# A delta-rule attention with a gated feed-forward: first feed-forward tiles in plain fp32, weights unpacked with byte copies, 32-blocks solved whole

## The chip, the cores and the metric

The kernel runs on one core of a Trainium2 chip. PE is TensorE, DVE is VectorE, ACT is ScalarE, POOL is GpSimd and SP is the engine that issues most transfers. The metric is the device time of one execution, in microseconds. The time before is the median of three runs; one more execution was profiled, and its page, trace and rows by line are what the text quotes. The prediction's sum is made against the profiled execution.

## The reference

The kernel computes two things in a row. The first is a delta-rule recurrence for 4 x 8 heads of 768 steps and width 48. The second is a feed-forward layer over the 3072 resulting tokens (width 384), with a hidden width of 2048.

```python
k_n = k / (np.linalg.norm(k, axis=-1, keepdims=True) + 1e-06)
for t in range(S):
    y[:, :, t] = np.einsum('bhd,bhde->bhe', q[:, :, t], state)
    v_old = np.einsum('bhde,bhd->bhe', state, kt)
    state = state + bt[:, :, :, None] * np.einsum('bhd,bhe->bhde', kt, vt - v_old)
# x: y laid out as (tokens, 384)
h = x @ w_in                                   # 384 -> 2048
g = where(h >= 1, h, where(h <= -1, 0.0, (h + 1) ** 2 / 4))
out = g @ w_out                                # 2048 -> 384
```

The two weight matrices arrive in 64-bit floating point; q, k, v and beta are 32-bit.

## The kernel before, in words

The sequence is cut into twelve chunks of 64 steps; two chunks form a group, so there are six groups G = 0 to 5. Within a chunk the recurrence becomes a triangular system. `gram_k` and `gram_q` form products of keys with keys and of keys with queries. `lanes` transposes the diagonal 32-blocks so that each of the 128 partitions holds one block, computes the norms and scales. A solve then inverts the blocks on DVE, one column after another, and an `unlanes` routine transposes them back. In groups 0 and 1 (`G < WHOLE`) the solve works on two 16-blocks at once (`solve`, 15 steps), and `merge16_a` and `merge16_b` join them on PE; from group 2 on `solve_whole` (30 steps) inverts 32-blocks. `merge32_a` and `merge32_b` join 32-blocks to 64. The chain over chunks is `chain_r` (read the state), `chain_u` (solve for the updates), `chain_y` (outputs, which become the x of the feed-forward layer) and `chain_d` (update the state).

The feed-forward layer is worked off in items `(G, f, bs)`: f is one of sixteen tiles of 128 hidden units, bs says which of the group's two chunks the item covers (256 columns each). An item is an up-projection (`up`, PE, result h), a gate (ACT and DVE, result s), a split of s into a rounded high half and a low half (`rest`, results ghi and glo), and a down-projection (`down`, PE, result o, two items later). Weights and activations are held as a high and a low half in the type fp32r, and each product is three passes (`PASSES`: high x high, high x low, low x high). Group 0 begins with six items on the first chunk alone (`LEAD`), goes on with ten on both, and ends with six on the second chunk.

The 64-bit weights are turned into fp32 on the chip by `weight(f)`, per tile and half: ACT scales the upper words (L149), POOL multiplies by zero what is left of them in place (L150), DVE shifts and joins words (L152, L154), ACT rounds to the high half (L158), DVE subtracts to get the low half (L160). Ten tiles are loaded at the start (`HOLD`), six later.

The order of the work is written out by hand. The opening, before the first item, is a list of `stage(...)` calls with weight steps filled in (`run(wu, n)`); while DVE solves, PE runs `KEEP` dummy matmuls (L518, plain fp32, 512 columns). From the first item on, `plan(G)` puts each piece of the next group's recurrence at a place counted in items from the group's start: `at(pe, G, t, ...)` for products on PE, `at(fill, G, t, ...)` for steps of the generators and loads. All engines work off their instructions in the order in which they are issued. x reaches its place partly by transfers from a staging tile (`stg`, six per chunk), issued by SP, for chunk 0 half of them by ACT.

The gate before, in the loop over items (relu is ACT; max is DVE):

```python
relu(s[:, c], h[:, c], half, -0.5)
relu(s[:, c], s[:, c], one, -1.0)
nc.scalar.activation(out=s[:, c], in_=s[:, c], func=AF.Square)
nc.vector.tensor_tensor(out=s[:, c], in0=h[:, c], in1=s[:, c], op=ALU.max)
```

Of the kernel before, what the change touches and what calls it, by code (L numbers as in the profile page):

```python
# [22 lines left out]
KEEP = 18  # L23
PASSES = ((0, 0), (0, 1), (1, 0))
WHOLE = 2
HOLD = 10
LEAD = 6
LAG = 2


@with_exitstack
def delta_rule_moe(ctx: ExitStack, tc: tile.TileContext, kqa, kqb, kv, beta, w, out):
# [88 lines left out]
    weight_loads(2, HOLD)  # L121
# [20 lines left out]

    def weight(f):

        x = X4[:, f % 4]
        st = RAW.pop(f)
        sti, xi = st.bitcast(I32), x.bitcast(I32)
        h, l = (sti[:, :, k::2] for k in (1, 0))
        nc.scalar.mul(out=x, in_=st[:, :, 1::2], mul=2.0 ** -112)  # L149
        nc.gpsimd.tensor_scalar(out=st[:, :, 1::2], in0=st[:, :, 1::2], scalar1=0.0, scalar2=None, op0=ALU.mult)  # L150
# [3 lines left out]
        nc.vector.scalar_tensor_tensor(out=xi, in0=xi, scalar=3, in1=l, op0=ALU.logical_shift_left, op1=ALU.bitwise_or)  # L154
# [3 lines left out]
        nc.scalar.copy(out=hi, in_=x)  # L158
        yield
        nc.vector.tensor_tensor(out=lo, in0=x, in1=hi, op=ALU.subtract)  # L160
        yield


# [70 lines left out]
    ZT = XT[:, :, :, 0:32]  # L234

    def lanes(G):

        A = S["A"] = sb.tile([P, 32, 32], F32, name="A", bufs=1)
        if G < WHOLE:
            X = S["X"] = sb.tile([P, 2, 16, 16], F32, name="X", bufs=1)  # L240
            Xf = X.rearrange("l s c t -> l (s c t)")
# [22 lines left out]
        if G >= WHOLE:  # L264
            nc.vector.scalar_tensor_tensor(out=A, in0=A, scalar=-1.0, in1=gm[:, :, None].broadcast_to([P, 32, 32]), op0=ALU.mult, op1=ALU.mult)  # L265
            nc.gpsimd.affine_select(out=A, in_=A, pattern=[[-1, 32], [1, 32]], base=0, channel_multiplier=0,  # L266
                                    compare_op=ALU.is_gt, fill=0.0)
            nc.gpsimd.memset(A.rearrange("l c t -> l (c t)")[:, 0:1024:33], 1.0)
            return
        A16 = S["A16"] = sb.tile([P, 2, 16, 16], F32, name="A16", bufs=1)  # L270
        for s in range(2):
            b = slice(16 * s, 16 * s + 16)
            nc.vector.tensor_tensor(out=A16[:, s], in0=A[:, b, b], in1=gm[:, b, None].broadcast_to([P, 16, 16]), op=ALU.mult)
        X32 = S["X32"] = sb.tile([P, 32, 32], F32, name="A", bufs=1)
        nc.gpsimd.memset(X32, 0.0)
        yield

    def solve():

        X, A16 = S["X"], S["A16"]  # L280
        for j in range(15):
# [2 lines left out]
            nc.vector.tensor_tensor(out=pr, in0=X[:, :, 0:n, j:j + 1].broadcast_to([P, 2, n, m]),  # L284
                                    in1=A16[:, :, j:j + 1, j + 1:16].broadcast_to([P, 2, n, m]), op=ALU.mult)
            nc.vector.tensor_tensor(out=X[:, :, 0:n, j + 1:16], in0=X[:, :, 0:n, j + 1:16], in1=pr, op=ALU.subtract)
# [493 lines left out]
```

## Time and profile before

| what | value |
|---|---|
| median of 3 runs | 640.39 us (640.23 to 642.42) |
| profiled execution | 640.92 us |
| its span | 639.2 us |
| mean granted PE clock | 0.946 |
| PE, DVE, ACT, POOL busy | 582.3, 451.9, 387.6, 101.6 us |
| first up-projection of group 0, 1, 2 | at 73.15, 213.81, 299.83 us |
| first up-projection of group 5 | at 566.50 us |

The span is what the trace covers, from the first instruction to the last; the execution's time is 1.7 us longer. In a view of stretches, each row gives the stretch's length and then each engine's busy time with the number of instructions, the granted clock of PE as a share of full speed, the DMA engines' share and GB/s. In a view of groups by line, a row gives the busy time in all and the mean of one in nanoseconds, then the engine's idle time just before such instructions and what ended it. In a timeline, a row gives the start and the length; a bracket gives the idle time before it and what ended that. Each plain fp32 matmul shows as two records.

### The profile page before, as it was taken

The page shows a single profiled execution, that of the slowest core. Times are in us where ns is not written, and L with a number is a line of the kernel's source. Part 1 is how long each engine was busy: PE and PEld are TensorE (multiplying, and loading weights), DVE is VectorE, ACT ScalarE, POOL GpSimd, SP SyncE. Part 2 cuts the span into 40 slices and gives each one's busy share as a digit, 9 for nine tenths or more (in the row PEclk, how much of TensorE's full clock was granted, in tenths as well). Part 3 has the DMA queues.
Part 4 walks back from the last instruction along what each step waited for, and adds up shares of the span by engine and source line. Part 5 has one row for each costly group of instructions (what it writes and reads, how often), then busy time and mean ns, then how long its engine had stood idle before and what let it go on. Part 6 is the DMA issues. An engine that isn't in the chain of part 4 may idle for free.

```text
span 639.2 us, 21003 instructions
## 1 busy us (share of the span) xinstructions
PE 582.3 (91%) x9158; PEld 499.8 (78%) x9158; DVE 451.9 (71%) x921; ACT 387.6 (61%) x696; POOL 101.6 (16%) x119
## 2 busy tenths in 40 slices
PE   9944588897988999999999999999999999999996
PEld 7443477676877787888987888978888878899995
DVE  6999479795486598785897866997948973533332
ACT  4145567753664766656766657656667577566663
POOL 3458525300000400001200004000012000000000
PEclk9955689697999999999999999999999999999998
DMA  7914353000014210015210043200052000010002
GB/s 241 417 48 151 120 184 110 1 26 3 4 28 125 84 50 28 2 40 168 73 31 4 2 121 90 74 27 4 24 147 79 11 3 2 19 45 14 1 2 49
DMA packets 21100, 42.35 MB, mean 66 GB/s; under 512 B 4624, under 2 KB 10128, under 8 KB 21008
## 3 DMA queue, kind: packets, MB, share of 16 engines
q1 hardware_dynamic: 20144, 40.14, 20.4%
q8 instruction: 72, 1.18, 0.8%
q10 hardware_dynamic: 608, 0.79, 0.4%
q0 software_dynamic: 256, 0.08, 0.1%
q14 instruction: 20, 0.16, 0.1%
HBM read 33.91 MB, written 4.72 MB: 60 GB/s over the span
## 4 chain that ended last, share of the span: by engine, by line
PE 53%; DVE 32%; ACT 6%; issue 5%; DMA 1%; ACTq 0%; POOL 0%; SPq 0%; DVEq 0%
PE o L583 20%; PE h L568 18%; PE ch L175 8%; DVE glo L693 4%; DVE pr L295 3%; DVE A L297 3%; DVE s L723 3%; PE ch L420 3%; PE ch L358 2%; ACT ghi L692 2%; DVE wt L152 2%; ACT WQ L200 2%; DVE xb L154 2%; DVE pr L284 1%; DVE XT L305 1%
## 5 line engine op out<-in xcount | busy, mean ns | idle before, releaser
L568 PE MATMUL h<-xb,wt 128*128 128x512 f32 (+1 forms) x918 | 227.0, 392 | 9.3 <-DVE s L723 4.8
L583 PE MATMUL o<-wt,ghi 128*128 128x384 f32 x768 | 202.8, 346 | 0.8 <-ACT ghi L692 0.8
L568 PEld LDWEIGHTS h<-xb,wt 128*128 128x128 f32 x918 | 165.6, 192 | 42.4 <-DVE s L723 6.4
L583 PEld LDWEIGHTS o<-wt,ghi 128*128 128x128 f32 x768 | 138.1, 190 | 8.3 <-ACT ghi L692 1.5
L583 PE MATMUL o<-wt,glo 128*128 128x384 f32 x384 | 130.8, 341 | 0.0
L723 DVE TENSOR_TENSOR s<-h,s 128x512 f32<-128x512 f32 (+1 forms) x102 | 66.8, 655 | 89.6 <-ACT s L715 89.1
L692 ACT CAST ghi<-s 128x512 fp32r<-128x512 f32 (+1 forms) x102 | 60.8, 596 | 87.1 <-DVE s L723 77.6
L693 DVE TENSOR_TENSOR glo<-s,ghi 128x512 fp32r<-128x512 f32 (+1 forms) x102 | 68.7, 673 | 47.4 <-ACT ghi L692 46.0
L697 ACT ACTIVATE s<-h,half 128x512 f32<-128x512 f32 (+1 forms) x102 | 67.4, 661 | 50.7 <-PE h L568 50.0
L583 PEld LDWEIGHTS o<-wt,glo 128*128 128x128 f32 x384 | 73.0, 190 | 0.9 <-DVE glo L693 0.9
L697 ACT ACTIVATE s<-s,one 128x512 f32<-128x512 f32 (+1 forms) x102 | 71.4, 700 | 2.4
L715 ACT ACTIVATE s<-s 128x512 f32<-128x512 f32 (+1 forms) x102 | 61.9, 607 | 3.2
L208 POOL TENSOR_SCALAR_AFFINE_SELECT WQ<-WQ 64x512 f32<-64x512 f32 x48 | 34.2, 712 | 95.8 <-ACT WQ L200 93.3
L150 POOL TENSOR_SCALAR wt<-wt 128x768 f32<-128x768 f32 x16 | 39.2, 2454 | 41.6 <-ACT xb L149 41.2
L297 DVE TENSOR_TENSOR A<-A,pr 128x30 f32<-128x30 f32 (+14 forms) x120 | 40.9, 341 | 4.4
L295 DVE TENSOR_TENSOR pr<-A 128x30 f32<-128x30 f32 (+14 forms) x120 | 40.1, 334 | 1.4
L266 POOL TENSOR_SCALAR_AFFINE_SELECT A<-A 128x1024 f32<-128x1024 f32 x4 | 5.1, 1268 | 200.4 <-DVE A L265 200.4
L404 ACT COPY SU<-ch 64x384 f32<-64x384 f32 x46 | 21.8, 473 | 14.8 <-PE ch L175 14.1
L200 ACT COPY WQ<-ch 64x512 f32<-64x512 f32 x40 | 23.2, 580 | 7.4 <-PE ch L175 6.6
L420 PEld LDWEIGHTS ch<-WQ,SU 112*64 112x64 f32 x704 | 21.6, 138 | 4.6 <-ACT SU L404 3.4
L456 DVE TENSOR_TENSOR SU<-ch,SU 48x384 f32<-48x384 f32 x40 | 22.2, 555 | 3.4 <-PE ch L175 2.7
L420 PE MATMUL ch<-WQ,SU 112*64 112x64 f32 x704 | 23.1, 224 | 1.1 <-ACT SU L404 1.1
(130 smaller groups left out, 617.1 us busy)
## 6 DMA issues: line engine op xcount, KB each, us to landing
wt<-in_w_dram SPq DMA_DIRECT2D x16, 768.0 KB, 7.9
KV<-in_kv_dram SPq DMA_DIRECT2D x24, 384.0 KB, 4.5
out_dram<-wx SPq DMA_DIRECT2D x47, 96.0 KB, 2.2
WQ<-in_kqb_dram SPq DMA_DIRECT2D x24, 128.0 KB, 3.2
WK<-in_kqb_dram SPq DMA_DIRECT2D x24, 96.0 KB, 3.5
WQ<-in_kqa_dram SPq DMA_DIRECT2D x22, 96.0 KB, 2.8
xb<-X SPq DMA_DIRECT2D x63, 32.0 KB, 2.0
WK<-in_kqa_dram SPq DMA_DIRECT2D x20, 96.0 KB, 3.4
```

The lines of the kernel that those rows point to most:

```text
L150: nc.gpsimd.tensor_scalar(out=st[:, :, 1::2], in0=st[:, :, 1::2], scalar1=0.0, scalar2=None, op0=ALU.mult)
L175: nc.tensor.matmul(tiles[i][dst:dst + l.shape[-1], v], l, r, start=True, stop=True)
L295: nc.vector.tensor_tensor(out=pr, in0=A[:, 0:n, j:j + 1].broadcast_to([P, n, m]), in1=A[:, j:j + 1, j + 1:32].broadcast_to([P, n, m]), op= ...
L297: nc.vector.tensor_tensor(out=A[:, 0:n, j + 1:32], in0=A[:, 0:n, j + 1:32], in1=pr, op=ALU.add)
L420: nc.tensor.matmul(yy[tk:tk + C, v // NP, v % NP], SF[rows, u:u + C], w_[rows, h, v, :], start=True, stop=True)
L568: nc.tensor.matmul(h[:, cols(bs)], WT[f][:, 0, x, k * P:(k + 1) * P], XB[G][:, y, k, cols(bs)], start=(n == 0), stop=(n == 8))
L583: nc.tensor.matmul(oacc[G, k], (ghi, glo)[x][:, k * P:(k + 1) * P], WT[f][:, 1, y, :], start=(new and n == 0), stop=(left[G, b] == 0 and n ...
L692: nc.scalar.copy(out=ghi[:, c], in_=s[:, c])
L693: nc.vector.tensor_tensor(out=glo[:, c], in0=s[:, c], in1=ghi[:, c], op=ALU.subtract)
L697: nc.scalar.activation(out=out, in_=in_, func=AF.Relu, bias=bias, scale=scale)
L715: nc.scalar.activation(out=s[:, c], in_=s[:, c], func=AF.Square)
L723: nc.vector.tensor_tensor(out=s[:, c], in0=h[:, c], in1=s[:, c], op=ALU.max)
```

## The change

- **Plain fp32.** The first eight tiles (`PLAIN = 8`), for the items of group 0 that cover the first chunk or both, multiply fp32 weights `W32` with fp32 x (`X32`) in one plain product instead of three passes; their s goes to the down-projection as it is. `split_x` later makes the high and low halves of group 0's x, and `rework` those of the eight tiles (a copy, a rounding, a subtraction each), from the tenth item on.
- **Unpacking.** `parts(f)` is three ACT operations: the top three bits of the lower word by way of its highest byte, a byte copy of sign and exponent, and the scaling of the upper word. `words(f)` is two DVE operations. POOL's pass is gone. All sixteen tiles are loaded at the start; `parts` of twelve of them (`HOLD = 12`) are issued in one row before the first solve.
- **Solve.** Every group uses the 32-block solve; the 16-block routines are gone. Before it stand a scaling of the whole tile on DVE and two POOL operations.
- **Gate.** One relu, the square, and one DVE operation of two steps (min with 1, max with h).
- **Pieces.** `chain_d(0)`, `chain_r(1)` and loads of group 2 move from the first items into the opening. The places of all pieces are new lists (`FIRST`, `OPEN`, `SECOND`, `STEADY`), the solve of a group is spread over its own stretch (`spread`), and `PRE` and `PACE` say how many weight steps run where. `KEEP` grows from 18 to 26.
- **Smaller things.** `merge32_b` gives its first two evictions to ACT and its last two to DVE instead of taking turns; the zeroing of XT is done once, by POOL; `copy` with `ONE` (all zeros) leaves the copies on DVE.

The diff, cut to its core:

```diff
-KEEP = 18
+KEEP = 26
-WHOLE = 2
-HOLD = 10
+HOLD = 12
+PLAIN = 8
...
-    weight_loads(2, HOLD)
+    weight_loads(2, FT)
...
+    def parts(f):
+        st = RAW[f]
+        by, wd = st.bitcast(U8), st.bitcast(I32)
+        nc.scalar.activation(out=wd[:, :, 0::2], in_=by[:, :, 3::8], func=AF.Identity, bias=floor, scale=2.0 ** -5)
+        nc.scalar.copy(out=by[:, :, 3::8], in_=by[:, :, 7::8])
+        nc.scalar.mul(out=st[:, :, 1::2], in_=st[:, :, 1::2], mul=2.0 ** -112)
+    def words(f):
+        wd = RAW[f].bitcast(I32)
+        rest_, top = wd[:, :, 0::2], wd[:, :, 1::2]
+        nc.vector.tensor_scalar(out=rest_, in0=rest_, scalar1=7 - 2 ** 31, scalar2=None, op0=ALU.bitwise_and)
+        yield
+        y = RAW[f][:, :, 0:DM] if f < PLAIN else X2[:, f % 2]
+        nc.vector.scalar_tensor_tensor(out=y.bitcast(I32), in0=top, scalar=3, in1=rest_, op0=ALU.logical_shift_left, op1=ALU.bitwise_or)
+        W32[f] = y
+        yield
+    def halves(f, x):
+        both_ = const.tile([P, 2, 2, DM], F32R, name=f"wt{f}")
+        hi, lo = (both_[:, :, i, :] for i in range(2))
+        nc.scalar.copy(out=hi, in_=x)
+        yield
+        nc.vector.tensor_tensor(out=lo, in0=x, in1=hi, op=ALU.subtract)
...
+    def rework():            # per tile f < PLAIN: copy to x = X2[:, f % 2], then halves(f, x)
+                nc.vector.tensor_copy(out=x, in_=W32[f])
...
+    def split_x():           # per k: high half on ACT, low half on DVE
...
+    PRE = [0, 0, 2, 0, 0, 1, 4, 2, 2]
...
+    for f in range(HOLD):
+        parts(f)
     run(solve())
     run(unlanes())
-    stage(one_(merge16_a, 0), (wu, 3))
...
+    run(wu, next(W))
+    stage(one_(merge32_a, 0), (sv[0], 2), (wu, next(W)))
+    stage(one_(merge32_a, 1), (wu, next(W)))
     late_q()
+    stage(one_(merge32_b, 0), (wu, next(W)))
+    stage(one_(merge32_b, 1), (sv[1], 2), (wu, next(W)))
+    stage(one_(chain_u, 0), (wu, next(W)))
+    stage(both(chain_y, 0), (wu, next(W)))
     load_k(2)
     load_q(2)
+    stage(one_(chain_d, 0), (wu, next(W)))
+    load_kv(2)
+    stage(one_(chain_r, 1), (wu, next(W)))
+    load_k(3)
...
+    def plain(G, f, bs):
+        return G == 0 and f < PLAIN and bs != (1,)
...
+            if plain(G, f, bs):
+                nc.tensor.matmul(h[:, cols(bs)], W32[f][:, 0, k * P:(k + 1) * P], X32[:, k, cols(bs)], start=(k == 0), stop=(k == 2))
+                continue
...
+    FIRST = dict(ln=[3.5, 3.5, 4.0, 4.0, 4.5, 5.0, 5], so=[6.0, 10], un=[10.5, 11.0, 11.5, 12.0], va=[7.5, 7.5], vb=[12.0, 13.5], r=[7.5], m=[12, 12, 13, 13], kt=[7.5], K=[14, 15.0], T=[17.0, 18, 18.5, 19, 19.5, 20, 20.5], Q=[21.5, 23.5])
+    OPEN = dict(I=[0, 0.5, 1, 1.5, 2, 6.5, 6.0], L=[2.5, 2.5], X=[2.0, 2.5, 3.5, 4.5, 4.5, 5.0], W=[10.0, 0.5])
+    SECOND = dict(ln=[-7.5, -6.5, -6.0, -4.5, -3.5, -3.5, -3.0], so=[-2.5, 5.0])
+    STEADY = dict(ln=[-5.5, -5, -5, -4.0, -4.0, -2.5, -2.5], so=[-0.5, 5.0], un=[5.5, 6.0, 6.0, 6.5], va=[2.0, 5.0], vb=[9.0, 10.0], r=[9.0], m=[8, 8.5, 8.5, 9.5], kt=[7.5], K=[10, 10.5], T=[11.0, 11.5, 12.0, 12.5, 13.0, 13.5, 15.5], Q=[17.0, 18.0])
...
-        relu(s[:, c], h[:, c], half, -0.5)
+        relu(s[:, c], h[:, c], half, 0.5)
...
-        relu(s[:, c], s[:, c], one, -1.0)
+        run(wu, pace(n, 0))
...
-        nc.vector.tensor_tensor(out=s[:, c], in0=h[:, c], in1=s[:, c], op=ALU.max)
+        nc.vector.scalar_tensor_tensor(out=s[:, c], in0=s[:, c], scalar=1.0, in1=h[:, c], op0=ALU.min, op1=ALU.max)
```

`PACE` gives the weight steps before and after each item's square: 5, 2 for the first item, mostly 2, 2 after it; by it all sixteen tiles are in words before the ninth item.

More of the change, by code (lines that the diff above doesn't have):

```diff
@@ L160, in weight, with unpack @@
         nc.vector.tensor_tensor(out=lo, in0=x, in1=hi, op=ALU.subtract)
+        WT[f] = both_
         yield
+    def unpack():
+        last = None
+        for f in range(FT):
+            if HOLD <= f + 1 < FT:
+                parts(f + 1)
+            yield from words(f)
+            if f >= PLAIN:
+                split = halves(f, W32.pop(f))
+                next(split)
+                if last:
+                    next(last)
+                yield
+                last = split
+        if last:
+            next(last)
+    def rework():
+        last = None
+        for f in range(PLAIN + 1):
+            if f < PLAIN:
+                x = X2[:, f % 2]
+                nc.vector.tensor_copy(out=x, in_=W32[f])
+                W32.pop(f)
+                split = halves(f, x)
+            if last:
+                next(last)
+                yield
+                next(last)
+            yield
+            last = split
+    def split_x():
+        XB[0] = sb.tile([P, 2, 3, 2 * NB], F32R, name="xb")
+        for k in range(3):
+            nc.scalar.copy(out=XB[0][:, 0, k], in_=X32[:, k])
+            yield
+            nc.vector.tensor_tensor(out=XB[0][:, 1, k], in0=X32[:, k], in1=XB[0][:, 0, k], op=ALU.subtract)
+            yield
     pairs = ((0, C, C, 0), (C, 0, 0, 1))
@@ L520, in delta_rule_moe @@
     run(ln)
+    for q, r in enumerate(QS):
+        for x in range(2):
+            nc.gpsimd.dma_start(out=beta_sb[r + 16 * x:r + 16 * x + 16, 1:NS, :], in_=beta[q:64:4, 2 + x:ntot:2, :])
+    for f in range(HOLD):
+        parts(f)
     run(solve())
@@ L573, in down @@
         ghi, glo = gs.pop((G, f, bs))
+        passes = [((ghi, glo)[x], WT[f][:, 1, y]) for x, y in PASSES] if glo else [(ghi, W32[f][:, 1])]
         for b in bs:
@@ L581, in down @@
                     new = False
-                for n, (x, y) in enumerate(PASSES):
-                    nc.tensor.matmul(oacc[G, k], (ghi, glo)[x][:, k * P:(k + 1) * P], WT[f][:, 1, y, :],
-                                     start=(new and n == 0), stop=(left[G, b] == 0 and n == 2))
+                for n, (x, y) in enumerate(passes):
+                    nc.tensor.matmul(oacc[G, k], x[:, k * P:(k + 1) * P], y, start=(new and n == 0),
+                                     stop=(left[G, b] == 0 and n == len(passes) - 1))
     def store(G, b):
@@ L655, in plan, with steps @@
-        if G < NS - 2:
-            at(fill, G, L, (load_kt, b + 2))
-            at(fill, G, R + 0.5, (load_k, a + 2))
-            at(pe, G, K[0], one(gram_k, a + 2))
-            at(pe, G, K[1], one(gram_k, b + 2, KT))
+        p, q = (STEADY if G else FIRST), (FIRST, SECOND, STEADY)[min(G, 2)]
+        def steps(gen, ts):
+            for t in ts:
+                at(fill, G, t, (gen, 1))
+        steps(lanes(G + 1), q["ln"])
+        spread(G, solve(), *q["so"])
+        steps(unlanes(), p["un"])
@@ new lines, in plan @@
+        steps(scale_v(a), p["va"])
+        steps(scale_v(b), p["vb"])
+        if G == 0:
+            I = OPEN["I"]
+            at(pe, G, I[0], one(chain_u, 1))
+            at(pe, G, I[1], *both(chain_y, 1))
+            at(pe, G, I[2], one(chain_d, 1))
+            for t, f, g in zip(I[3:], (gram_k, gram_k, gram_q, gram_q), (a, b, a, b)):
+                at(pe, G, t, one(f, g))
+            at(fill, G, OPEN["L"][0], (load_q, 3))
+            at(fill, G, OPEN["L"][1], (load_kv, 3))
+            steps(split_x(), OPEN["X"])
+            rw, (t, d) = rework(), OPEN["W"]
+            steps(rw, [t + int(j * d * 2) / 2 for j in range(2 * PLAIN + 1)])
```

255 lines of the change are left out of this document (70 added, 185 removed).

## The prediction

> **What bounds the kernel now.** I read the page's head first, then the busy times by stage, cut where the work changes hands.
>
> ```profile
> span 639.2 us, 21003 instructions
> ```
>
> ```profile
> 31.09:45.08 13.99, 6.81 (x512) 6.39 (x512) 13.75 (x16) 6.47 (x9) 7.77 (x3) 0.62 0.20 79
> 45.08:59.45 14.37, 5.95 (x258) 4.77 (x259) 13.99 (x19) 7.76 (x15) 11.30 (x11) 0.50 0.32 101
> 59.45:73.15 13.70, 6.54 (x126) 5.87 (x127) 10.64 (x18) 7.38 (x15) 9.84 (x8) 0.62 0.43 136
> ```
>
> ```profile
> 73.15:213.81 140.66, 119.84 (x2491) 102.51 (x2491) 98.42 (x203) 80.98 (x161) 28.23 (x32) 0.90 0.24 70
> ```
>
> ```profile
> 213.81:299.83 86.02, 84.48 (x1287) 73.16 (x1285) 67.84 (x148) 56.24 (x102) 7.47 (x13) 1.00 0.15 45
> 299.83:388.72 88.89, 87.69 (x1361) 76.06 (x1361) 70.12 (x152) 58.49 (x106) 8.81 (x14) 1.00 0.20 57
> ```
>
> The columns are length, then busy time of PE, PE weight load, DVE, ACT and POOL, the granted clock and the DMA share. Three regimes show. Up to 73.15 us, the opening, PE waits and runs at a clock of 0.50 to 0.62, while DVE is busy 13.75 of 13.99 us. The first group (73.15 to 213.81) takes 140.66 us with nobody full: PE 119.84 at a clock of 0.90, DVE 98.42. From 213.81 on PE is full; group 2 idles 88.89 - 87.69 = 1.2 us. So a gain must come from the opening and the first group; in the later groups only about 1 us each is to be had. The first three stages are cut where the 16-block merge (31.09), the 32-block merge (45.08) and the state update of chunk 0 (59.45) begin on PE. Next, the places of the opening that the change touches, in the timeline:
>
> ```profile
> 73.15 0.98 PE L568 MATMUL h<-xb,wt 128*128 128x256 f32 x3 [4.21 <-DMA xb<-X]
> ...
> 75.92 1.53 PE L175 MATMUL ch<-SU,KV 64*48 64x48 f32 x64
> ...
> 81.36 1.01 PE L568 MATMUL h<-xb,wt 128*128 128x256 f32 x3
> ```
>
> ```profile
> 22.57 0.92 ACT L149 ACTIVATE xb<-wt 128x768 f32<-128x768 f32 x1 [4.48 <-DMA wt<-in_w_dram]
> ```
>
> ```profile
> 61.98 0.82 ACT L158 CAST wt<-xb 128x768 fp32r<-128x768 f32 x1
> 63.59 0.92 ACT L149 ACTIVATE xb<-wt 128x768 f32<-128x768 f32 x1 [0.79 <-ACT wt L158]
> ```
>
> The first up-projection starts at 73.15 (after 4.21 us of waiting for x), the second at 81.36. ACT's first weight pass over tile 2 starts when that tile lands, at 22.57.
>
> **The change part by part.** Durations come from the groups by line, shown where they are used.
>
> *Whole solve in the opening.*
>
> ```profile
> L297 DVE TENSOR_TENSOR A<-A,pr 128x30 f32<-128x30 f32 (+14 forms) x120 | 40.9, 341 | 4.4
> L295 DVE TENSOR_TENSOR pr<-A 128x30 f32<-128x30 f32 (+14 forms) x120 | 40.1, 334 | 1.4
> ```
> ```profile
> L284 DVE TENSOR_TENSOR pr<-X,A 128x30 f32<-128x30 f32 (+7 forms) x30 | 9.6, 318 | 0.8
> ```
> ```profile
> L305 DVE STREAM_TRANSPOSE XT<-A 128x1024 f32<-128x1024 f32 x4 | 9.0, 2257 | 0.0
> L286 DVE TENSOR_TENSOR X<-X,pr 128x30 f32<-128x30 f32 (+7 forms) x30 | 8.2, 274 | 1.0
> ```
> ```profile
> L303 DVE TENSOR_TENSOR A<-A,gm 128x1024 f32<-128x1024 f32 x4 | 4.9, 1218 | 0.0
> ```
> ```profile
> L266 POOL TENSOR_SCALAR_AFFINE_SELECT A<-A 128x1024 f32<-128x1024 f32 x4 | 5.1, 1268 | 200.4 <-DVE A L265 200.4
> ```
>
> ```profile
> 16.35 0.76 DVE L273 TENSOR_TENSOR A<-A,gm 128x256 f32<-128x256 f32 x2
> ```
>
> The four later solves show the whole form, the first two the form in halves. A whole solve costs (40.9 + 40.1)/4 = 20.25 us of DVE, the two-half solve (9.6 + 8.2)/2 = 8.9, so +11.35. It starts about 2 us later: one full-tile scaling (about 1.2, as L303) and POOL's masking (1.27) stand ahead of it instead of 0.76 us of scaling at 16.35. From about 19.2 us, with gaps of 0.03 between 60 instructions, the solve ends near 41.3. The scaling and the big transpose (1.22 + 2.26) follow, so PE can merge at 44.8, against 45.08 now: the longer solve costs what the dropped 16-block merge (13.99 us of stage) gives back. Alone that is a wash; but DVE's unpacking in those 14 us is displaced too.
>
> *Byte copies on ACT.*
>
> ```profile
> L149 ACT ACTIVATE xb<-wt 128x768 f32<-128x768 f32 x16 | 14.4, 907 | 12.3 <-DVE wt L160 7.0 <-DMA wt<-in_w_dram 4.5 <-ACT wt L158 0.8
> ```
> ```profile
> L158 ACT CAST wt<-xb 128x768 fp32r<-128x768 f32 x16 | 13.2, 826 | 2.3 <-DVE xb L154 2.3
> ```
> ```profile
> L150 POOL TENSOR_SCALAR wt<-wt 128x768 f32<-128x768 f32 x16 | 39.2, 2454 | 41.6 <-ACT xb L149 41.2
> ```
>
> Each tile now takes three ACT operations of 768 elements, twelve tiles stand in ACT's queue ahead of the merge's evictions, and whoever waits for those waits for all of them. No row shows a byte access with a step. Bounds: 826 ns (L158, nothing strided) below; 2454 (POOL's pass over such a tile, the furthest row) above. I take L149's 907, the nearest: same engine, elements and step of eight bytes. Tile 2 lands at 22.57, so tile 11 is done at 22.57 + 10 x 3 x (0.907 + 0.03) = 50.7; I take 50, as independent operations overlap slightly. ACT, not the solve, sets when the merge goes on.
>
> [...]
>
> *From the merge to the first up-projection.* Four evictions, the second half of the merge and its own evictions take about 5 us (now 59.45 - 45.08 = 14.4 with weight work and POOL's masking in between), so the chain of group 0 starts at 55 (now 59.45). From there to the second up-projection takes 81.36 - 59.45 = 21.9 us now. Out of it fall: the first item's own up, 75.92 - 73.15 = 2.8; the 4.21 us of waiting for x, which the state update and the read of group 1 now fill, moved ahead of the first item; and ACT's two weight operations at 61.98 and 63.59, 1.7, which no longer exist for the first tiles. 21.9 - 8.7 = 13.2, so the first item starts at 68.2, with two pieces done that now come after it. The loads of group 2 (SP's queue) and the beta loads (POOL's queue) move up as well; the weight loads are all issued ahead of them and end near 45 at the pace seen, before x is moved, so I cost them at nothing; if they were late, tile 11 and the 50 would be.
>
> *First group, DVE.* Now 98.42 us busy. The unpacking inside it:
>
> ```profile
> 73.15:213.81 140.66, 5.71 (x6) 0.90 0.24 70
> ```
> ```profile
> 73.15:213.81 140.66, 7.10 (x7) 0.90 0.24 70
> ```
> ```profile
> 73.15:213.81 140.66, 7.59 (x8) 0.90 0.24 70
> ```
>
> These are L152, L154 and L160 alone: 20.4 us. Three more durations:
>
> ```profile
> L154 DVE SCALAR_TENSOR_TENSOR xb<-xb,wt 128x768 int32<-128x768 int32 x16 | 15.9, 992 | 0.2
> ```
> ```profile
> L371 DVE COPY XT<-XT 32x512 f32<-32x512 f32 x24 | 11.5, 480 | 0.2
> ```
> ```profile
> L693 DVE TENSOR_TENSOR glo<-s,ghi 128x512 fp32r<-128x512 f32 (+1 forms) x102 | 68.7, 673 | 47.4 <-ACT ghi L692 46.0
> ```
>
> By `PRE` the opening will have done 11 of the 32 word steps. Left, at 0.95 for each (in the stage the 21 operations above took 20.4/21 = 0.97): 21 x 0.95 = 20.0, the 16 low halves 15.2, and eight copies of the plain weights, 0.7 each (L371's 480 ns per 512 elements): 40.8, so +20.4. The solve adds 11.35 and its ends 1.3; splitting x 2.1 (three as L693). Off: the 16-block merge 2.2 (two transposes of half L305's size, 1.1 each at most, and two short subtractions, an estimate), the low halves of eight gate results 4.7 (six are half as wide), x's low half and group 1's read 3.3 (an estimate: six operations of 384 columns and two of 128, at L693's rate). Sum 98.4 + 20.4 + 11.35 + 1.3 + 2.1 - 2.2 - 4.7 - 3.3 = 123.3 us. DVE's fullest stages run 97% (13.99 of 14.37); with some waits between engines I take 96%: 128 us. The first step of the words has one tensor operand; bounded by L154 (0.99) and by L371's rate (0.72), I take 0.95, the nearer form.
>
> [...]
>
> *Plain fp32 on PE.*
>
> ```profile
> 17.55 13.04 PE L518 MATMUL ch<-SU 128*128 128x512 f32 x30
> ```
> ```profile
> 305.31 2.26 PE L568 MATMUL h<-xb,wt 128*128 128x512 f32 x9
> 307.41 0.51 PE L583 MATMUL o<-wt,ghi 128*128 128x384 f32 x2
> ...
> 309.49 0.85 PE L568 MATMUL h<-xb,wt 128*128 128x512 f32 x3
> ```
>
> A plain matmul is two records of 13.04/30 = 0.435, so 0.87 per 512 columns; three split ones take 2.10/3 = 0.70. Two full and six half-wide tiles: 2 x 1.0 + 6 x 0.5 = 5 us more PE time, not less. What pays is what stands beside it. It is hidden: PE's share of the first group is 119.84 x 0.90 = 108 us of full clock; less the 16-block merge (6.81 us of PE in the opening at a clock of 0.62, so 4), two pieces moved out and one moved on (about 1.3 each; the row at 75.92 shows 1.53 at a lowered clock, so 3.9), plus 5, makes 105, under DVE's 128. Without that cover it costs its 5.
>
> *Gate in three operations.* One ACT operation less per item:
>
> ```profile
> L697 ACT ACTIVATE s<-s,one 128x512 f32<-128x512 f32 (+1 forms) x102 | 71.4, 700 | 2.4
> ```
>
> 71.4 us of ACT in all; the DVE operation keeps two tensors and, as I take it, its time. ACT is not the bound, so I count no time for it; it buys 0.7 us of slack per item.
>
> *Pieces laid anew.*
>
> ```profile
> PE ch L358 <- DVE XT L305: 5.1, 4, 1.5
> ```
>
> PE's one wait per later group is the merge behind the transpose. The new places put 1.5 f-tiles between them, so it goes. Late next is the gate: the solve now runs in 5.5 f-tiles, 20.25/5.5 = 3.7 us of DVE per f-tile plus 1.35 for the gate and its low half (twice L693), 5.0 against PE's 4.18 (305.31 to 309.49 above). Through the transposes DVE falls some 3 us behind; with two items between up and down, about 4 us are free. I take a net gain of 0.5 for each of three groups, and 1.2 for group 1 (its idle 1.54, and some late starts, against a piece of 1.3 moved into it).
>
> **Sum.** The first group ends at 68.2 + 128 = 196.2 instead of 213.81: -17.6. Later groups -1.2 - 1.5. Together -20.3 on the profiled 640.92: 620.6, or 620 by the median of 640.39, 0.5 lower.
>
> **Rivals.** *Byte copies are dear (slower).* ACT's strided byte operations stand at the one place where all wait. Twenty of them lie behind tile 2's landing; the gain of 20 is gone when each takes 0.907 + 1.0 = 1.9 us. At POOL's 2.454 the opening grows by 31, so 640 + 11 = 651. For it: no row shows the access. Against it: L149's step costs only 907 - 826 = 81 ns. Chance 0.08.
>
> *DVE overfull in the later groups.* If the slack does not hold, PE waits the 3 us or so in each of four groups instead of gaining 0.7: +14, 634. For it: 5.0 against 4.2 per f-tile. Against it: now DVE runs near full beside the solve without stalling PE. Chance 0.17.
>
> *The first group packs better.* With POOL's 39.2 us gone, collisions shorten (L154 and its kind), words run at L371's rate and waits vanish: DVE 118 at 98%, 120 us, and an opening 3 us shorter: 609. Chance 0.15.
>
> **How the numbers follow.** My forecast has 0.60, itself 611 to 630: DVE 98% to 90% full in the first group (126 to 137 us), ACT's operations and the words' first step at their lower bounds. The range of 606 to 637 takes in most of the second and third rival and leaves out the first. Under 0.5%, or 3.2 us, a measurement here tells nothing. Faster: 0.60 + 0.15 + 0.12 = 0.87; same 0.05, from the second rival's tail; slower 0.08.
>
> **What would show it.** Right: the first up-projection within 66 to 71 us, ACT's three weight operations back to back from 16 to about 50 with PE idle behind them; DVE over 90% busy from there to about 196; the wait of the merge for the transpose gone; last group unchanged. Wrong: byte operations well over 0.95 us; PE waiting for DVE's gate in the first half of the later groups; or a first group over 140 us, DVE idle behind ACT.

## The result, and the profile after

The changed kernel takes 655.69 us (median of 4 runs, 655.4 to 655.9) against 640.36 (4 runs) before: ratio 1.0231, 95% interval 1.021 to 1.0252. It is slower by 2.3%, where 3.2% faster was predicted. (Two corrections to what stands ahead: the first up-projection of group 5 before stood at 561.54 us, and 566.50 lies within that group's second item; and the work of chunk 0 that begins at 59.45 is `chain_u`, which solves for the updates, not the update of the state.)

The page's head and the busy times by stage of the changed kernel, columns as before. The cuts are the second half of the 32-block merge (61.83), the first up-projection of groups 0, 1, 2 and 3; the first row begins where the first half of the merge begins.

```profile
span 654.0 us, 18782 instructions
```

```profile
45.69:61.83 16.14, 1.93 (x129) 1.80 (x129) 5.11 (x10) 15.86 (x15) 0.00 (x0) 0.50 0.02 6
61.83:79.72 17.89, 13.98 (x385) 12.10 (x385) 9.08 (x16) 9.11 (x23) 0.00 (x0) 0.60 0.15 41
79.72:216.98 137.26, 114.06 (x1744) 89.34 (x1743) 120.01 (x240) 78.11 (x140) 8.59 (x12) 0.90 0.16 45
216.98:303.84 86.86, 85.59 (x1285) 72.93 (x1285) 66.13 (x139) 46.90 (x89) 7.00 (x10) 1.00 0.19 55
303.84:395.83 91.99, 89.06 (x1369) 75.98 (x1361) 73.06 (x152) 47.15 (x89) 7.21 (x10) 1.00 0.20 54
```

Read against the same cuts of before (by the starts of the first up-projections): opening +6.6 us (79.72 against 73.15), first group -3.4, group 1 +0.8, groups 2 and 3 +3.1 each, group 4 +4.6 (88.50 against 83.85), group 5 unchanged at 77.7. The sum, 14.8, is the difference of the spans. So two things were lost, one in the opening and one in the later groups, and the first group won little.

*The opening.* From 45.69 to 61.83 us PE does 1.93 us of work and ACT 15.86 of 16.14. The timeline says what PE waits for, and the groups by shape, cut to 14 to 62 us, say what ACT does:

```profile
45.69 1.08 PE L350 MATMUL ch<-XT,GG 32*32 32x32 f32 x64 [9.23 <-DVE XT L335]
...
60.64 0.88 ACT L151 ACTIVATE wt<-wt 128x768 f32<-128x768 f32 x1
61.42 1.16 ACT L359 ACTIVATE GG<-ch 32x256 f32<-32x256 f32 x3
...
61.83 0.71 PE L350 MATMUL h<-GG 32*32 32x32 f32 x4 [14.21 <-ACT GG L359]
...
79.72 2.93 PE L550 MATMUL h<-xb,wt 128*128 128x256 f32 x6
```

```profile
L150 ACT COPY wt<-wt 128x768 uint8<-128x768 uint8 x12 | 23.3, 1945 | 0.4
L149 ACT ACTIVATE wt<-wt,floor 128x768 int32<-128x768 uint8 x12 | 11.9, 990 | 0.0
L151 ACT ACTIVATE wt<-wt 128x768 f32<-128x768 f32 x12 | 10.9, 910 | 0.4
```

The merge's first half runs at 45.69, when the solve is ready. Its eviction (L359) stands on ACT behind the twelfth tile's L151 and starts at 61.42. Of a tile's 3.85 us, half is the byte copy L150: 1945 ns, twice an operation of the same 768 elements in 32 bits (910).

*The later groups.* The waits of PE in group 2 (303.84 to 395.83):

```profile
PE h L553 <- DVE s L707: 2.1, 4, 0.8
PE o L569 <- DVE glo L675: 0.6, 1, 0.6
```

The wait for the transpose is gone, as predicted, and PE waits for DVE's gate instead. It does so in the first eight f-tiles (an f-tile is the stretch from the start of one item's up-projection to the next; they are counted from 0 in each group, and the first group has 22). The eight end at 344.00; the first row below covers all but the last microsecond of them, with DVE busy 37.25 of 39.16 us. The second row is the same eight f-tiles of the kernel before, which took 36.06 us with PE never idle:

```profile
303.84:343.00 39.16, 36.69 (x301) 31.45 (x294) 37.25 (x82) 17.75 (x30) 5.78 (x8) 1.00 0.23 62
```

```profile
299.83:335.89 36.06, 36.06 (x298) 32.13 (x298) 31.23 (x74) 25.07 (x41) 6.07 (x10) 1.00 0.26 73
```

Over the whole group PE idles 2.9 us instead of 1.2. The trace books the other 1.4 of the 3.1 us as busy time of PE (89.06 against 87.69), with the same products to do; why these take longer there it does not show.

### The profile page after: what moved, and what is told of

Same layout as the page of the kernel before. It is cut to its first block, busy times and chain, and to the rows that moved or that the text cites. A ratio compares the mean times of both kernels' runs of the same rounds, so it can differ in the third digit from the quotient of the medians.

```text
span 654.0 us, 18782 instructions
## 1 busy us (share of the span) xinstructions
PE 584.1 (89%) x8106; PEld 484.9 (74%) x8106; DVE 470.5 (72%) x959; ACT 359.9 (55%) x617; POOL 50.1 (8%) x74
## 4 chain that ended last, share of the span: by engine, by line
PE 46%; DVE 33%; ACT 14%; issue 5%; ACTq 0%; DVEq 0%
PE o L569 17%; PE h L553 15%; DVE pr L325 7%; DVE A L327 7%; PE ch L227 7%; ACT wt L150 4%; DVE glo L675 3%; DVE s L707 3%; PE ch L410 3%; ACT wt L149 2%; ACT wt L151 2%; DVE GG L231 2%; DVE XT L335 2%; PE ch L350 1%; DVE SU L457 1%
## 5 line engine op out<-in xcount | busy, mean ns | idle before, releaser
L553 PE MATMUL h<-xb,wt 128*128 128x512 f32 (+1 forms) x846 | 213.2, 396 | 10.5 <-DVE s L707 10.2
L569 PE MATMUL o<-wt,ghi 128*128 128x384 f32 x744 | 196.9, 347 | 0.0
L553 PEld LDWEIGHTS h<-xb,wt 128*128 128x128 f32 x846 | 152.4, 189 | 46.7 <-DVE s L707 16.0
L707 DVE SCALAR_TENSOR_TENSOR s<-s,h 128x512 f32<-128x512 f32 (+1 forms) x97 | 64.0, 659 | 72.9 <-ACT s L699 72.4
L679 ACT ACTIVATE s<-h,half 128x512 f32<-128x512 f32 (+1 forms) x97 | 64.8, 668 | 68.3 <-PE h L553 63.3
L327 DVE TENSOR_TENSOR A<-A,pr 128x30 f32<-128x30 f32 (+9 forms) x180 | 66.4, 369 | 6.6
L325 DVE TENSOR_TENSOR pr<-A 128x30 f32<-128x30 f32 (+9 forms) x180 | 65.1, 362 | 5.7 <-POOL A L314 1.4
L150 ACT COPY wt<-wt 128x768 uint8<-128x768 uint8 x16 | 31.2, 1952 | 0.5
L550 PE MATMUL h<-xb,wt 128*128 128x256 f32 (+1 forms) x48 | 22.2, 619 | 5.0 <-DVE s L707 3.0
L410 PE MATMUL ch<-WQ,SU 112*64 112x64 f32 (+1 forms) x736 | 25.2, 227 | 1.1 <-ACT SU L394 1.1
L410 PEld LDWEIGHTS ch<-WQ,SU 112*64 112x64 f32 (+1 forms) x736 | 23.6, 141 | 3.5 <-issue 3.2
L255 ACT COPY WQ<-ch 64x512 f32<-64x512 f32 x40 | 23.2, 580 | 3.4 <-PE ch L227 2.7
## 6 DMA issues: line engine op xcount, KB each, us to landing
wt<-in_w_dram SPq DMA_DIRECT2D x16, 768.0 KB, 14.3
```

The costliest lines, as they stand in the source:

```text
L150: nc.scalar.copy(out=by[:, :, 3::8], in_=by[:, :, 7::8])
L325: nc.vector.tensor_tensor(out=pr, in0=A[:, 0:n, j:j + 1].broadcast_to([P, n, m]), in1=A[:, j:j + 1, j + 1:32].broadcast_to([P, n, m]), op= ...
L327: nc.vector.tensor_tensor(out=A[:, 0:n, j + 1:32], in0=A[:, 0:n, j + 1:32], in1=pr, op=ALU.add)
L410: nc.tensor.matmul(yy[tk:tk + C, v // NP, v % NP], SF[rows, u:u + C], w_[rows, h, v, :], start=True, stop=True)
L553: nc.tensor.matmul(h[:, cols(bs)], WT[f][:, 0, x, k * P:(k + 1) * P], XB[G][:, y, k, cols(bs)], start=(n == 0), stop=(n == 8))
L569: nc.tensor.matmul(oacc[G, k], x[:, k * P:(k + 1) * P], y, start=(new and n == 0), stop=(left[G, b] == 0 and n == len(passes) - 1))
```

## The experiments

Times of runs are given as ratios to the kernel before, run beside them; group lengths and starts are read from the starts of the first up-projections in each run's timeline. Five traces share the opening and the first group unchanged (the changed kernel, e2, e3, e6, e9): their first up-projections stand between 79.7 and 81.1 us, and their first groups take 136.8 to 137.9. Smaller differences than these say nothing.

**The byte copy by itself (e1_forms).** Each branch is set on one line here.

```diff
+        hw = st.bitcast(mybir.dt.uint16)
+        if f % 4 == 0:   nc.scalar.copy(out=by[:, :, 3::8], in_=by[:, :, 7::8])
+        elif f % 4 == 1: nc.scalar.copy(out=hw[:, :, 1::4], in_=hw[:, :, 3::4])
+        elif f % 4 == 2: nc.scalar.copy(out=by[:, :, 3::8], in_=wd[:, :, 0::2])
+        else:            nc.scalar.copy(out=by[:, :, 0:384], in_=by[:, :, 7::8])
```

> The changed kernel, with ScalarE's byte copy in four forms, tile by tile (f mod 4): as it is, bytes with a step of 8 to bytes with a step of 8; 16-bit words with a step of 4 (the same bytes and their neighbours, which are masked out later, so the weights stay right); 32-bit words with a step of 2 to bytes with a step of 8; bytes with a step of 8 to bytes in a row. In the last two the sign and exponent bits of the weights are lost. Theory, that the writing of single bytes with a step is dear: 1.95 us for the first and third form, about 0.95 us for the fourth, and the 16-bit form between them. Rival, that the reading of bytes is dear: 1.95 us for the first and fourth, 0.95 us for the third. Six of twelve tiles about 1 us shorter would bring the first up-projection from 79.7 to about 74 us and the time to 650 us.

The groups by shape of this run, from 14 to 62 us (L152, L154, L156, L158 are the four forms in the order of the diff):

```profile
L154 ACT COPY wt<-wt 128x768 uint16<-128x768 uint16 x3 | 5.9, 1967 | 0.1
L152 ACT COPY wt<-wt 128x768 uint8<-128x768 uint8 x3 | 5.9, 1963 | 0.1
L156 ACT CAST wt<-wt 128x768 uint8<-128x768 int32 x3 | 5.9, 1952 | 0.1
L158 ACT COPY wt<-wt 128x768 uint8<-128x768 uint8 x3 | 2.6, 878 | 0.1
```

Reading bytes with a step is cheap (878, against the 826 of L158 before, where nothing has a step). Writing them with a step doubles the operation (1963 from bytes, 1952 from 32-bit words), and 16-bit words written with a step are no better (1967), which I had put in between. Only three of the twelve tiles are short, so the first up-projection comes at 76.63 us, not the 74 I had expected; the time, from one run, is 652.25 us.

**The predicted price (e5_byte_row).** All sixteen byte copies take the fourth form.

> The changed kernel, with ScalarE's byte copy of all 16 tiles written to bytes in a row (0.88 us in the run of the forms) instead of every eighth byte (1.95). The copied bytes land elsewhere, so the weights lose sign and exponent bits; the number of operations and elements stays. This is the price that the prediction took. Theory, that the price of this one operation is the error of the opening: twelve tiles end 13 us earlier, at about 48.5 us, the first up-projection comes at 66 to 68 us, the first group is 1 to 4 us shorter, time 638 to 642. Rival, that the step from merge to first up-projection was mis-sized as well: first up-projection at 72 us or later, time over 646.

Timeline and, below it, the groups of ACT from 14 to 52 us:

```profile
50.11 1.56 ACT L359 ACTIVATE GG<-ch 32x256 f32<-32x256 f32 x4
...
68.41 2.93 PE L550 MATMUL h<-xb,wt 128*128 128x256 f32 x6
```

```profile
L150 ACT COPY wt<-wt 128x768 uint8<-128x768 uint8 x12 | 10.7, 893 | 0.4
```

At 893 ns per copy the merge's eviction starts at 50.11 (predicted: 50) and the first up-projection comes at 68.41 (predicted: 68.2). Ratio 1.0028 (1.0011 to 1.0044), against 1.0231 with the stepped write; of the two traces this one is 11.0 us shorter, by one operation's write pattern alone. The time, 643.51, lies just over the 638 to 642 that I expected: the first group stays at 137.5 us, where I had expected 1 to 4 us less, so shorter byte copies do not shorten it.

**Fewer tiles in the opening (e4_hold8, e10_hold10).** `HOLD = 8` with `PACE = [5, 0] + 8 * [0, 3] + [1]`, and, on top of e2_old_places, `HOLD = 10`.

> The changed kernel, with 8 instead of 12 tiles unpacked by ScalarE in the opening, the others one per f-tile in the first group from its second f-tile on. Theory, that the queue of ScalarE's unpacking (12 tiles of 3.85 us) sets when the merge goes on: first up-projection 15.4 us earlier, at about 64 us; the first group gets 4 x 3.85 us of ScalarE work more, which stretches it by 3 to 8 us; time 643 to 649. Rival, that the merge waits for something else (VectorE's words, the clock, a load): first up-projection at 77 to 80 us, time 655 to 662.

> The kernel of e2_old_places with 10 instead of 12 tiles unpacked by ScalarE in the opening; the places of the other word steps are untouched. Theory: first up-projection 2 x 3.85 = 7.7 us earlier than there, at 72 to 73 us, first group 138 to 140 us, time 638 to 640. Rival, that the first group takes it all back: first group over 143 us, time 643 or more.

First up-projection at 67.19 us with 8 tiles and 73.22 with 10; first group 142.6 and 141.2 us. Ratios 1.0133 (1.0089 to 1.0178) and 0.9985 (0.9972 to 0.9999). ACT's queue does set the opening. With 8 tiles the gain is 12.5 of the 15.4 us taken from the queue, and the first group takes back 5.4; the time, 648.81, lies within the 643 to 649 expected. With 10 it takes back 3.5 of 7.6 against e2_old_places; neither bracket of mine, 138 to 140 or over 143, held that, and the time, 640.91, is just over the 638 to 640 of the theory.

**The later groups: which of the new places costs (e2_old_places, e3_grams_early, e6_long_late, e9_short_only).** The lists of places alone differ. The changed kernel has the solve short (`so=[-0.5, 5.0]`) and the query products late (`Q=[17, 18]`).

```diff
-    STEADY = dict(ln=[-5.5, -5, -5, -4.0, -4.0, -2.5, -2.5], so=[-0.5, 5.0], un=[5.5, 6.0, 6.0, 6.5], va=[2.0, 5.0], vb=[9.0, 10.0], r=[9.0], m=[8, 8.5, 8.5, 9.5], ...
+    STEADY = dict(ln=[-5.5, -5, -5, -4.5, -4.5, -4.5, -4.0], so=[-3.5, 7.0], un=[7.0, 7.5, 8.0, 8.5], va=[3.0, 4.0], vb=[8.0, 8.5], r=[6.0], m=[8, 8.5, 9, 9.5], kt=[5.0], K=[10, 10.5], T=[11.5, 12.0, 12.5, 13.0, 13.5, 14.0, 14.5], Q=[15.0, 16.0])
```

e2 is this diff; e3 changes only Q to `[15, 16]`; e6 is e2 with Q left at `[17, 18]`; e9 is e2 with only `ln`, `so` and `un` left as in the changed kernel. In all four the solve beside group 1 keeps the places of `SECOND`, so only from group 2 on are e2's places those of before.

> The changed kernel, with the pieces of the later groups (solve, gram products, merges, chain) at the places of the kernel before; opening and first group untouched. Theory, that the new places (solve in 5.5 f-tiles, the masks of the query products inside it) cost 3.1 + 3.1 + 4.7 us in groups 2 to 4: these groups return to about 88.9, 88.9 and 84 us and the time to 645 us. Rival, that the operations themselves (three-operation gate, merge evictions, more POOL work) are slower: groups stay at 92.0, 92.0 and 88.5 us, time 655.

> The changed kernel, with only the two query gram products of the later groups moved from f-tiles 17 and 18 to 15 and 16, so that POOL's masks of them no longer run beside the solve. Theory A, that POOL's masks beside the solve stretch VectorE's operations (7 operations of 0.7 to 0.85 us instead of 0.4): groups 2 to 4 shorter by about 2 us each, time 649. Theory B, that the compression of the solve into 5.5 f-tiles alone does it: within 1 us of 655.7.

> The changed kernel, with the later groups at the places of the kernel before but the two query gram products, with POOL's masks, left at f-tiles 17 and 18. Theory A, that the short spread of the solve (5.5 f-tiles) lengthens the groups: groups 2 and 3 stay at 88 to 89 us, time 645 to 647. Theory B, that the products and masks among the solve do it: 90.5 to 92 us, time 650 to 655.

> The kernel of e2_old_places (later groups at the places of before) with only the solve and what feeds and follows it (lanes, solve, unlanes) at the places of the changed kernel: the solve in 5.5 f-tiles from half an f-tile before the group. Theory, that the short spread alone overfills VectorE: groups 2 and 3 at 90.5 to 92 us, group 4 at 86.5 to 88.5, time 651 to 656. Rival, that the places of merges, chain and read count: groups 2 and 3 stay at 88 to 89 us, time 645 to 647.

Group 2 of each in a row of its stretch, for e2 and e9 with PE's largest wait in it. e2_old_places:

```profile
306.67:394.77 88.10, 87.79 (x1361) 76.11 (x1361) 69.78 (x152) 47.66 (x90) 6.65 (x11) 1.00 0.20 55
```

```profile
PE ch L350 <- DVE XT L335: 0.3, 1, 0.3
```

e3_grams_early:

```profile
306.36:399.18 92.82, 89.69 (x1364) 76.38 (x1361) 71.36 (x153) 47.21 (x89) 6.67 (x11) 1.00 0.19 53
```

e6_long_late:

```profile
305.18:393.37 88.19, 87.71 (x1362) 75.99 (x1361) 69.97 (x153) 47.58 (x89) 6.85 (x10) 1.00 0.20 56
```

e9_short_only:

```profile
306.41:398.98 92.57, 89.24 (x1362) 75.85 (x1361) 72.79 (x152) 46.98 (x90) 6.66 (x11) 1.00 0.19 53
```

```profile
PE h L553 <- DVE s L707: 3.3, 4, 1.3
```

With the solve over 10.5 f-tiles group 2 takes 88.1 to 88.2 us, with the solve over 5.5 it takes 92.0 to 92.8, wherever the query products and the other pieces stand. Ratios: e2 1.0066 (1.0042 to 1.009), e6 1.0041 (1.0027 to 1.0056), e3 1.028 (1.0246 to 1.0315), e9 1.0244 (1.0225 to 1.0263). The wait for the gate is there in e9 and gone in e2. So the short spread is the cause, together with the places of what feeds and follows the solve (`ln`, `un`), which moved with it in every run. Group 4 goes the same way: 88.5 us in the changed kernel, 87.1 in e9, 83.1 in e2 and 84.7 in e6. e2 (645.27 us) and e6 (644.68) came out about as their theories had it, e9 a little over its bracket (657.69). Group 1 is another matter: 86.03 us before, 86.86 in the changed kernel, 88.11 in e2; what it pays for, no run here tries apart.

Theory A of e3 fell; theory B's figure, within 1 us of 655.7, was missed too, at 659.06. Theory A came from this picture of the changed kernel (POOL's masks, then DVE's solve before, beside and after them):

```profile
312.22 2.88 POOL L263 TENSOR_SCALAR_AFFINE_SELECT WQ<-WQ 64x512 f32<-64x512 f32 x4 [13.76 <-ACT WQ L255]
```

```profile
311.43 0.35 DVE L327 TENSOR_TENSOR A<-A,pr 128x184 f32<-128x184 f32 x1
...
312.30 0.81 DVE L325 TENSOR_TENSOR pr<-A 128x198 f32<-128x198 f32 x1
313.14 0.70 DVE L327 TENSOR_TENSOR A<-A,pr 128x198 f32<-128x198 f32 x1
...
316.77 0.37 DVE L325 TENSOR_TENSOR pr<-A 128x220 f32<-128x220 f32 x1
```

These operations take 0.70 to 0.81 us beside the masks, where operations a little smaller and larger, just before and after, take 0.35 and 0.37. But moving the masks took 1.7 us off DVE in group 2 (73.06 to 71.36) and nothing off the group (91.99 to 92.82). The f-tiles that had the products got shorter by 1.3 us each, those that received them longer by 1.6 and 2.2.

**The gate alone (e7_gate3).** The kernel before, with the three-operation gate.

> The kernel before, with only the gate in three operations. Theory, that ScalarE is nowhere the bound: within 0.5% of before (637 to 643). Rival, that in the first group, where nobody is full, ScalarE and VectorE wait for each other in turn and each dropped operation shortens the chain: first group 3 to 8 us shorter, time 632 to 637. The later groups at most 1 us shorter each.

Ratio 0.9942 (0.9921 to 0.9964): faster than before, by a little more than the 0.5% that the theory allowed, and the best of all runs here that compute the whole. The first group is unchanged (140.6 us), so the rival fell. Groups 2 and 4 are 0.9 and 0.6 us shorter, group 1 is 0.7 longer, and PE's wait for the transpose in group 2, 1.2 us before, is now:

```profile
PE ch L358 <- DVE XT L305: 0.3, 1, 0.3
```

The two traces differ by 0.7 us in all, the timed runs by 0.58%, or 3.7 us. The execution that was traced was the slowest of the six (640.19 us, median 638.57), so the trace does not show where the rest lies.

**The first group (e8_combo, e11_copy_act, e12_all3, e13_pace12, e14_pace10, e15_grams_9).** All stand on e2_old_places (first group 137.7 us). e8: `HOLD = 8`, `PACE = 10 * [0, 3] + [1]`. e11: rework's copy by `nc.scalar.copy`. e12: e11 and `HOLD = 10`. e13: `PACE = [5, 2, 2, 2, 2, 2, 2, 2, 1, 1, 0, 0, 0, 0, 0, 2, 1, 2, 2, 2]`. e14: e12 with `PACE = [5, 0, 0, 2, 0, 2, 0, 3, 0, 3, 0, 0, 0, 0, 2, 3, 2, 3, 2, 3]`. e15: the last two of `I` from 6.5, 6.0 to 9.5, 9.0.

> The changed kernel, with the later groups at the places of the kernel before, 8 tiles unpacked in the opening and the other eight one per f-tile over the first ten f-tiles, always in the second half of the f-tile. Theory (both causes are independent and add): first up-projection at 67 us, first group 137 to 142 us, groups 2 to 4 at 88.1, 88.1 and 83.1 us, time 632 to 637, under both kernels. Rival, that the first group takes back what the opening gives (ScalarE is late there): first group over 146 us, time over 640.

> The kernel of e2_old_places with the eight copies of the plain weights (rework, 0.55 us each on VectorE) moved to ScalarE, where such a copy takes 0.83 us. Theory, that the middle of the first group is bound by VectorE (busy 97% there): 8 x 0.55 = 4.4 us less on VectorE shorten the first group from 137.7 to 133.5 to 135.5 us, time 641 to 643. Rival, that waits between engines set the pace there: first group at 137 us or more, time 645 or more.

> The kernel of e2_old_places with both 10 tiles in the opening and the copies of the plain weights on ScalarE. If both theories hold, they add: first up-projection at 72 to 73 us, first group 135 to 137 us, time 634 to 637, under both kernels. If ScalarE becomes late in the first group (its unpacking of the remaining tiles and the copies on one queue), the first group is 140 us or more and the time over 640.

> The kernel of e2_old_places with no word step at all in the f-tiles 5 and 6 of the first group: the steps of tiles 13 to 15 (with ScalarE's unpacking of 14 and 15) moved to the f-tiles 7 to 9. Theory, that ScalarE's unpacking among the gate and the evictions of the query products there costs the first group its missing time (f-tiles 5 and 6 take 20.0 us): these two fall to 11 to 14 us, the first group from 137.7 to 129 to 133 us, time 637 to 641. Rival, that the work is only handed on: f-tiles 7 to 9 longer by as much, first group 136 us or more.

> The kernel of e12_all3 (10 tiles in the opening, copies of the plain weights on ScalarE) with the word steps one tile per f-tile, none in the f-tiles 5 and 6. Theory as for e13_pace12: first up-projection at 72 to 73 us, first group 130 to 135 us, time 629 to 635. Rival, that the first group is full whatever the order: 139 us or more, time 639 or more.

> The kernel of e2_old_places with the two query gram products of the first group, with ScalarE's eight evictions and POOL's masks, moved from the f-tiles 6 and 6.5 to 9 and 9.5. Theory, that these evictions, queued behind ScalarE's unpacking, hold PE in f-tile 6 (13.55 us): it falls to 8 to 10 us, the first group to 133 to 135 us, time 641 to 643. Rival, that the gate waits for VectorE there whatever PE's pieces: first group 137 us or more.

e8's theory fell and its rival held: the first group took 153.3 us, f-tiles 5 to 7 alone 38. There ACT's unpacking stood ahead of the next relu: in f-tile 6 the relu (L679) starts at 116.89, right behind a tile's last unpacking operation (L151, 0.88 us from 116.11), and PE then waits 8.1 us for ACT's evictions (L255). Ratio 1.0084 (1.0051 to 1.0116).

e11: first group 136.1, a gain of 1.6 where 4.4 us of DVE were moved, between the theory's bracket and the rival's; ratio 1.0042 (1.0027 to 1.0058). e12: first up-projection at 72.24, first group 140.1; ratio 0.9966 (0.9953 to 0.998). The two gains add up, but they are smaller than hoped: a first group of 140 us or more and a time over 640 (it is 640.24) are the figures I had given for a late ACT. It is still faster than both kernels, by a third of a per cent against before.

e13 and e15 moved work away from f-tile 6, which takes 13.54 us in e2. The rows of e13 are f-tile 6, f-tiles 9 to 11, and the whole first group:

```profile
114.74:123.93 9.19, 8.40 (x139) 4.40 (x139) 7.95 (x19) 7.69 (x11) 4.37 (x6) 0.81 0.01 2
133.56:163.74 30.18, 18.18 (x62) 13.52 (x60) 28.19 (x62) 13.68 (x19) 0.00 (x0) 0.83 0.00 1
...
80.70:220.07 139.37, 112.91 (x1744) 88.16 (x1743) 121.03 (x241) 78.39 (x140) 8.41 (x12) 0.91 0.16 45
```

F-tile 6 fell to 9.19 us, and f-tiles 9 to 11 grew from 19.96 to 30.18. In e15 f-tile 6 fell to 6.33 and f-tile 9 grew from 8.34 to 15.86; group 137.5. In e14 the group took 143.2. Ratios: e13 1.0089 (1.0058 to 1.012), e15 1.0061 (1.0037 to 1.0085), e14 1.0053 (1.0038 to 1.0069). In e13 and e14 the rival held, though in e13 the f-tiles that grew are 9 to 11, not 7 to 9 as it said. In e15 f-tile 6 fell as the theory had it, further even, and the group was no shorter. In all three the work is handed on.

**DVE's work taken away (e16_no_solve).** e2_old_places, with the solve left out in the first group.

```diff
-        spread(G, solve(), *q["so"])
+        if G:
+            spread(G, solve(), *q["so"])
```

> The kernel of e2_old_places without the 60 operations of the solve in the first group (for the blocks of group 1, which therefore stay unsolved): 22.1 us of VectorE less, all in the f-tiles 6 to 11, where VectorE is busy 97% of the time. Theory, that VectorE's work there sets the length: these six f-tiles take 45.0 us now and fall by 10 to 20 us (the lower end if PE at its lowered clock, or ScalarE's unpacking, takes over), the first group to 118 to 128 us, time 626 to 635. Rival, that chains between ScalarE, VectorE and PE set it: first group 133 us or more.

The first group in parts: f-tiles 0 to 5, 6 to 11, 12 to 17, 18 to 21. The changed kernel, whose first group is that of e2 within half a microsecond:

```profile
79.72:113.75 34.03, 25.88 (x374) 19.16 (x373) 27.24 (x43) 21.69 (x36) 0.00 (x0) 0.85 0.33 95
113.75:158.85 45.10, 36.45 (x288) 24.13 (x289) 42.74 (x97) 23.62 (x34) 7.17 (x10) 0.85 0.03 10
158.85:190.41 31.56, 30.17 (x575) 26.97 (x575) 30.72 (x50) 20.74 (x41) 0.00 (x0) 1.00 0.01 3
190.41:216.98 26.57, 21.57 (x510) 19.08 (x509) 19.30 (x53) 12.07 (x32) 1.43 (x2) 0.94 0.34 92
```

e16_no_solve:

```profile
79.82:113.60 33.78, 25.57 (x373) 18.79 (x372) 27.26 (x43) 21.68 (x36) 0.00 (x0) 0.85 0.32 98
113.60:152.02 38.42, 34.33 (x288) 23.07 (x289) 24.77 (x40) 25.53 (x36) 7.78 (x10) 0.87 0.04 12
152.02:181.91 29.89, 29.89 (x575) 26.74 (x575) 28.65 (x48) 20.50 (x41) 0.00 (x0) 1.00 0.01 2
...
79.82:208.20 128.38, 112.54 (x1743) 88.91 (x1743) 98.88 (x180) 78.63 (x139) 9.21 (x12) 0.89 0.17 49
```

21 us less of DVE's work shortened the group by 9.3 (137.70 to 128.38); 6.6 of it lie in f-tiles 6 to 11. The group ends between my two theories, just over the first one's 128, and the six f-tiles fell by less than its 10; the time, one run of each, is 635.95 us against 640.76 before. DVE does bind the middle, 95% and 97% busy in the second and third row of the changed kernel, but PE is right behind it: without the solve PE is busy 34.33 of 38.42 us and then 29.89 of 29.89.

## Why the prediction was wrong, step by step

Forecast and measurement differ by some 35 us. The sum was laid out as a first up-projection at 68.2, a first group of 128 and -2.7 in the later groups; measured were 79.72 (+11.5), 137.26 (+9.3) and +11.6 (+14.3).

- *Whole solve in the opening: right, as far as its end shows.* PE's merge began at 45.69, predicted 44.8.
- *Byte copies on ACT: the failed step, +11.5 us.* "I take L149's 907, the nearest" held for the reads and the 32-bit write (990 and 910), not for the byte write (1945). The slight overlap that I had counted on is there: the second tile's L149 starts at 19.61 us, 0.10 before the first tile's L151 ends (0.91 us from 18.80). Ten byte writes at 1.04 us too much are 10.4 of the 11.4 us by which the merge's eviction came late (61.42, predicted 50). The order of the argument was right, since e5 with the price assumed gives 50.11 and 68.41. The rival "Byte copies are dear", given 0.08, was half right: it wanted twenty operations at 1.9 us, and ten of them, the byte writes, took that while the ten byte reads did not. So it had 20 us lost where 11.5 were. The nearest row had the same engine, elements and step, but its step was on the reading side alone: L149 before wrote 32-bit elements in a row, and its 81 ns were no evidence for a write with a step.
- *From the merge to the first up-projection: right.* 18.3 us from the eviction at 61.42, and 18.3 in e5; predicted 18.2.
- *First group: the share of DVE failed, +9.3 us.* DVE's work came out at 120.01 us, predicted 123.3. The words' first step is the main difference: 555 ns for 768 elements, not 950, ten times in the first group. The rows, over the whole trace, in which the two operations with one tensor operand take 549 and 555 ns and the one with two takes 956:

```profile
L157 DVE TENSOR_SCALAR wt<-wt 128x768 int32<-128x768 int32 x16 | 8.9, 555 | 0.1
L160 DVE SCALAR_TENSOR_TENSOR xb<-wt 128x768 int32<-128x768 int32 x8 | 7.6, 956 | 0.2
L197 DVE COPY xb<-wt 128x768 f32<-128x768 f32 x8 | 4.4, 549 | 0.0
```

  But "I take 96%" was measured on full stages of the opening and laid over the whole group. It holds in f-tiles 6 to 17 (73.46 busy of 76.66). In the first six f-tiles and the last four DVE idles 6.8 and 7.3 us. That is 14.1 of its 17.3 idle us, where the prediction allowed about 5 in all. Its largest waits there are for ACT's square of the gate (3.2) and for products of PE (3.0) in the first six, and for ACT's rounding of s (4.5) in the last four. No run removes these waits, so what would shorten these f-tiles stays open. The collisions on which the rival "The first group packs better" counted do show in the kernel before: L152 takes 1.63 us at 43.07, beside POOL's L150 (2.88 us from 42.35), where its median is 0.95.
- *Plain fp32 hidden: not tried apart.* PE's busy time at full clock, 114.06 x 0.90 = 103, agrees with the 105 predicted, but e16 shows that this cover is thin: with 21 us less on DVE, PE is the next bound.
- *Gate at no time: wrong, to the good.* Alone, on the kernel before, it is worth 0.6% (e7).
- *Pieces laid anew: the other failed step, +14.3 us.* The wait for the transpose went, as predicted; "about 4 us are free" did not cover DVE's lag. The rate was right (5.0 us of DVE per f-tile against 4.18 of PE): in f-tiles 3 to 7 of group 2 DVE is busy 23.9 of 24.9 us. With it the rival "DVE overfull" was right: +14 against the forecast by its price, +14.3 measured (0.8 + 3.1 + 3.1 + 4.6 = 11.6 against before), though it had put the same loss on each of the four groups. e2, e6 and e9 show the cause in groups 2 to 4, the short spread of the solve. "Now DVE runs near full beside the solve without stalling PE" was true of the long spread, which the change gave up; I had used the kernel before as evidence for a rate that it did not have.

## What to carry to other kernels

Where an edit puts a new form of operation on a queue that everybody waits behind, price reads and writes apart, and let a rival with a turning point inside the bounds have a chance that the lack of a row deserves. Compare, f-tile by f-tile, the rate of work that an engine is given with the time of the engine that sets the pace: a rate above it is not absorbed by two items of slack when it lasts for five. A busy share taken from a full stage may be laid only over stretches that are full as well.

## What the runs showed of the hardware

In these kernels ScalarE wrote 8-bit and 16-bit elements with a step of 8 bytes at half the pace: 1945 to 1967 ns for 768 elements, against 910 for 32-bit elements with the same step and 878 for bytes in a row. Reading with that step cost little (878 and 907, against 826 with no step). The step is the same in all of these writes but the one in a row, so it does not tell 1945 ns from 910; among the writes with a step, the width of the element does.
